# The last output rows in three column pieces: 256, then twice 128

## The chip, the core and the metric

The kernel runs on one core of a Trainium2 chip. A core has a matrix engine (PE, with the loading of its stationary operand shown apart as PEld), a vector engine (DVE), an activation engine (ACT), a general engine (POOL) and a queue engine for transfers (SP). PE writes its products into the banks of an accumulator memory (PSUM). ACT and DVE copy them from there into the core's working memory, which here is called evicting. Transfers between that memory and the chip's DRAM are issued from the queues of SP, ACT or POOL and carried out by 16 DMA engines that all queues share.

The metric is the device time of one execution in microseconds (us). The kernel before takes 514.16 us, the median of 3 runs (514.08 to 514.75).

## The reference

For 8 batches of 8 heads, 576 positions and 64 features the attention keeps only the scores that are within tau = 0.02 of a row's largest one. Its output, seen as 4608 rows of 512 features, goes through two dense layers:

```python
scores = scale * np.matmul(q, k.transpose(0, 1, 3, 2))
thresh = np.max(scores, axis=-1, keepdims=True) - tau
scores = np.where(scores >= thresh, scores, -1e9)
attn = np.exp(scores - np.max(scores, axis=-1, keepdims=True))
attn = attn / (np.sum(attn, axis=-1, keepdims=True) + 1e-09)
x = np.matmul(attn, v)                # then as 4608 rows of 512
h = x @ w_in                          # 512 -> 2048
g = np.maximum(0.01 * h, h)
out = g @ w_out                       # 2048 -> 512, float32
```

Inputs and outputs are float32. The kernel works with float16 operands in most matrix products.

## The kernel before

The attention runs over 16 steps of two head pairs (c), each of 9 tiles of queries (t). An order written out by hand, a list of letters for each tile, says in which sequence a tile's scores, its row maxima, its masking and the work of neighbouring steps are issued. The two dense layers are cut into small units that wait in a list called units. Letters of the order take units from the front of that list (the function work), so that PE has dense products to do while the vector engines treat the scores. What is left in the list after the last tile is issued by the last line of the kernel, work(len(units)).

A batch has 576 rows of output. 512 of them are treated per batch (push_main): 16 units of the first layer with 512 rows as moving columns, then 4 groups of second products. The 64 rows that remain, the tail, are treated for two batches together (push_tail): 2 x 64 = 128 rows. With i = 0, four units (h_unit) make the first product and its leaky ReLU, four groups of 128 columns each, and ACT writes them into gE, a tile of 16 blocks (j) of 128 x 128. With i = 1, four units (out_mm) make the second product: 16 matrix products, one per j, with gE's block j as the stationary operand and the 512 columns of w_out's block j as the moving one, all accumulated in one bank of PSUM. Batches 6 and 7 (b0 = B - 2) have the last tail, and its second product is the last thing that PE does.

Three sets of buffers matter. bank() gives one of two PSUM banks with the tag u, in turn. The attention's scores use two pairs of banks with the tag s. In working memory new_osb() gives one of two tiles for output (tag o), and the attention has two buffers with the tag far. A buffer is given again only after the last reader or writer of its former contents is done, and the needed waits are put in by the framework.

The last tail's eviction and its two stores stand on lines 392 to 397 and 435 to 438. ACT evicts columns 0 to 255, DVE columns 256 to 511 of the same bank. Both halves lie in one output tile, and then two stores are issued, one from SP for the 64 rows of batch 6 and one from ACT for the 64 rows of batch 7. A store of 64 rows moves 64 runs of 2 KB, 128 KB in all.

Of the kernel before, what the change touches and what calls it, by code (L numbers as in the profile page):

```python
# [9 lines left out]
FP32 = mybir.dt.float32  # L10
FP16 = mybir.dt.float16
OP = mybir.AluOpType
AF = mybir.ActivationFunctionType
# [3 lines left out]
def kernel(  # L17
# [10 lines left out]
    nc = tc.nc  # L28
    B, H, S, D = q.shape
# [6 lines left out]
    NJ = d_ff // 128  # L36
# [5 lines left out]
    sb = ctx.enter_context(tc.tile_pool(name="sb", bufs=1))  # L42
    ps = ctx.enter_context(tc.tile_pool(name="ps", bufs=1, space=bass.MemoryType.PSUM))
# [7 lines left out]
    w_out16 = sb.tile([128, NJ, d_model], FP16, name="wout16")  # L51
    gM = sb.tile([128, NJ, 512], FP16, name="gM")
    gEs = [sb.tile([128, NJ, 128], FP16, name=f"gE{i}") for i in range(2)]
# [15 lines left out]
    def bank():  # L69
        return ps.tile([128, 512], FP32, tag="u", bufs=2, name="u")  # L70
# [52 lines left out]
    def filler(n):  # L123
        if n > 0:
            t = bank()
            for _ in range(n):
                nc.tensor.matmul(out=t[:, :], lhsT=gM[:, 0, 0:128], rhs=gM[:, 0, :], start=True, stop=True,  # L127
                                 skip_group_check=True)
# [5 lines left out]
    def take(fs):  # L134
        r = list(fs)
        fs.clear()
        return r

    def run(fs):
        for f in fs:  # L140
            f()
# [221 lines left out]
    def h_unit(N, xs, g_out, j0, nj):  # L363

        assert all(("w", (j0 + nj - 1) // 4 * 4 + i) in was for i in range(4))
        t = bank()
        for j in range(nj):
            for gi in range(NG):
                nc.tensor.matmul(  # L369
                    out=t[:, ts(j, N)], lhsT=w_in16[:, gi, ts(j0 + j, 128)], rhs=xs[gi],  # L370
                    start=(gi == 0), stop=(gi == NG - 1), skip_group_check=True,
                )
        nc.scalar.activation(out=g_out, in_=t[:, 0:nj * N].rearrange("p (j n) -> p j n", j=nj),  # L373
                             func=AF.Prelu, bias=0.0, scale=1.0, alpha=0.01)
# [3 lines left out]
    def out_mm(key, g_in, part, osb, half, store):  # L378

        if part == 0:  # L380
            ot[key] = bank()
        t = ot[key]
        assert all(("w", 16 + j) in was for j in range(part * 4, part * 4 + 4))
        for j in range(part * 4, part * 4 + 4):
            nc.tensor.matmul(  # L385
                out=t[:, :], lhsT=g_in(j), rhs=w_out16[:, j, :],
                start=(j == 0), stop=(j == NJ - 1), skip_group_check=True,
            )
        if part == 3:
            del ot[key]  # L390
            o = osb()
            if key == (B - 2, "t"):
                nc.scalar.activation(out=o[:, half, 0:256], in_=t[:, 0:256], func=AF.Copy, bias=0.0, scale=1.0)  # L393
                nc.vector.tensor_copy(out=o[:, half, 256:512], in_=t[:, 256:512])  # L394
            else:
                nc.scalar.activation(out=o[:, half, :], in_=t[:, :], func=AF.Copy, bias=0.0, scale=1.0)  # L396
            store(o)

    units = []

    def new_osb():
        return sb.tile([128, 2, 512], FP32, tag="o", bufs=2, name="osb")
# [27 lines left out]
    def push_tail(b0, i):  # L430

        xs = [xE[g][:, b0:b0 + 2, :] for g in range(NG)]
        gE = gEs[b0 // 2 % 2]

        def store(o):
            for e in range(2):
                eng = nc.scalar if e == 1 and b0 == B - 2 else nc.sync
                eng.dma_start(out=out[ds((b0 + e) * S + 512, 64), :], in_=o[ds(e * 64, 64), 0, :])
        for j in range(0, NJ, 4):
            if i == 0:  # L440
                units.append((1, lambda j=j: h_unit(128, xs, gE[:, j:j + 4, :], j, 4)))
            else:
                units.append((0, lambda part=j // 4: out_mm(
                    (b0, "t"), lambda j: gE[:, j, :], part, new_osb, 0, store)))

    def work(n):
        for _ in range(min(n, len(units))):
            units.pop(0)[1]()

    with tc.manual_schedule():  # L450
        nc.scalar.preload_act_table_set("natural_log_exp_and_others")
        for i, tail in ((0, 0), (1, 0), (0, 1), (1, 1)):
# [6 lines left out]
            out=sel[:, :, :], in0=I32[:, 0:18].unsqueeze(2).to_broadcast([128, 18, 64]),  # L459
# [43 lines left out]
        for c in range(NC + 1):  # L503
            last = c == NC
            for t in range(NT):
                step = c * NT + t
                cl = c if c < 5 else 6 - c % 2
                ph = c % 2 * 9 + t

                def push():  # L510
                    if c % 4 == 2 and c > 2:
                        push_tail(c // 2 - 3, 1)
                    push_main(c // 2 - 1)
                    if c % 4 == 0:
                        push_tail(c // 2 - 2, 0)
                    if last:
                        push_tail(c // 2 - 2, 1)
                def target(x):
                    return x * NT + (6 if x == 2 else 6)
                nx = c // 2 * 2  # L520
                if step >= target(nx) or c < 2 and 0:
                    nx += 2
                def count():
                    global_ = sum(share[i % 18] for i in range(step, max(target(nx), step + 1)))
                    return (len(units) - credit) * share[ph] / global_
                n = None
                for o in orders[cl][t].split():
                    if o == "G":
                        if c > 1 and c % 2 == 0:
                            push()  # L530
                            nx = c // 2 * 2 + 2
                        continue
                    if n is None:
                        credit = min(credit, 1.0) + count()
                        n = min(int(credit + 0.01), len(units))
                        credit -= n
                        k1 = min(n, max(0, (n + up[cl][t]) // 2))
                        heads = [u[0] for u in units[:n]]
                    if o == "f":
                        filler([[1, 2, 3, 3, 3, 2, 2, 2, 2], [1, 3, 3, 2, 3, 3, 2, 3, 2], [1, 1, 4, 3, 2, 1, 0, 1, 0]][cl][t] if cl < 3 else 0)  # L540
                    elif o == "S" and not last:
                        s_mm(c, t)
                    elif o[0] == "V" and c > 0:
                        values(c - 1, int(o[1]))
                    elif o == "0" and not last:
                        s_max(c, t, 0, tau_f <= 8.0 and (t in d0[cl]))
                    elif o == "1" and not last:
                        direct = tau_f <= 8.0 and (t in d1[cl] or c > 2 and t not in d1n[cl] and not any(heads))
                        s_max(c, t, 1, direct)
                    elif o == "d" and c > 0:  # L550
                        sums_0(c - 1)
                    elif o == "r" and c > 0:
                        sums_1(c - 1)
                    elif o == "x" and c > 0:
                        sums_2(c - 1)
                    elif o == "T" and c > 0:
                        sums_3(c - 1)
                    elif o == "U":
                        work(k1)
                    elif o == "u":  # L560
                        work(n - k1 - (1 if "w" in orders[cl][t] and n > k1 else 0))
                    elif o == "w":
                        work(1 if n > k1 else 0)
                    elif o[0] == "P":
                        pi = {"a": (2 * c + 2, 0), "b": (2 * c + 2, 1), "c": (2 * c + 3, 0), "d": (2 * c + 1, 1), "e": (2 * c + 1, 0), "f": (2 * c + 3, 1)}[o[1]]
                        if pi[0] < NP:
                            prep(*pi)
                    elif o == "h":
                        run(take(due))
                    elif o[0] == "Q" and c > 0:  # L570
                        sums_4(c - 1, int(o[1]))
                    elif o == "M":
                        if prev is not None:
                            s_mask(*prev)
                            prev = None
                        if not last:
                            prev = (c, t)
                    elif o == "L":
                        run(take(soon))
                for f in plan.get(step, ()):  # L580
                    f()
# [36 lines left out]
```

## Time and profile before

| what | value |
|---|---|
| median of 3 runs | 514.16 us |
| time of the profiled execution | 513.46 us |
| its span, first to last instruction | 511.7 us |
| busy: PE, PEld | 501.1 us (98%), 272.1 us (53%) |
| busy: DVE, ACT, POOL | 412.8 us (81%), 427.8 us (84%), 205.1 us (40%) |
| granted PE clock | 0.999 |
| last tail, first products (L369, 64 of 128 columns) | from 500.11 us, 3.57 us |
| last tail, second products (L385, 16 of 512 columns) | from 503.68 us, 3.47 us |
| its evictions, ACT (L393) and DVE (L394) | 383 ns and 424 ns |
| its stores, from issue to landing | 2.3 us (SP), 2.6 us (ACT) |

Times are those of one profiled execution, counted from the start of its span. In the lines of the profile L385 is line 385 of the kernel, and out<-in names the tile that is written and the tiles that are read. SPq and ACTq are instructions that a queue works off, among them the issue of a transfer. A busy time of PE is modelled at its end, since its products are pipelined: the start times of a row of products, rather than the duration of one, tell its pace. The DMA share of a stretch is the mean busy share of the 16 DMA engines.

### The profile page before, as it was taken

The page shows a single profiled execution, that of the slowest core. Times are in us where ns is not written, and L with a number is a line of the kernel's source. Part 1 is how long each engine was busy: PE and PEld are TensorE (multiplying, and loading weights), DVE is VectorE, ACT ScalarE, POOL GpSimd, SP SyncE. Part 2 cuts the span into 40 slices and gives each one's busy share as a digit, 9 for nine tenths or more (in the row PEclk, how much of TensorE's full clock was granted, in tenths as well). Part 3 has the DMA queues.
Part 4 walks back from the last instruction along what each step waited for, and adds up shares of the span by engine and source line. Part 5 has one row for each costly group of instructions (what it writes and reads, how often), then busy time and mean ns, then how long its engine had stood idle before and what let it go on. Part 6 is the DMA issues. An engine that isn't in the chain of part 4 may idle for free.

```text
span 511.7 us, 13929 instructions
## 1 busy us (share of the span) xinstructions
PE 501.1 (98%) x5155; PEld 272.1 (53%) x5155; DVE 412.8 (81%) x1084; ACT 427.8 (84%) x775; POOL 205.1 (40%) x471
## 2 busy tenths in 40 slices
PE   8899999999999999999999999999999999999996
PEld 5455554555555475555555475555555575545444
DVE  5888898998899889998999889998999889981000
ACT  3898978988998988999898988999898988983712
POOL 5554567533642346323642346323642346320000
PEclk9999999999999999999999999999999999999999
DMA  8999999998999899979997899978997899764112
GB/s 183 176 214 199 209 200 185 177 176 146 193 182 151 139 183 181 189 139 156 173 194 135 159 183 191 160 141 153 166 201 138 158 193 146 105 94 88 41 42 61
DMA packets 260547, 80.60 MB, mean 158 GB/s; under 512 B 248704, under 2 KB 257920, under 8 KB 260480
## 3 DMA queue, kind: packets, MB, share of 16 engines
q1 hardware_dynamic: 234032, 70.68, 78.5%
q0 software_dynamic: 26368, 8.92, 16.7%
q8 instruction: 40, 0.66, 0.6%
q14 instruction: 27, 0.22, 0.1%
q10 hardware_dynamic: 80, 0.13, 0.1%
HBM read 36.70 MB, written 9.44 MB: 90 GB/s over the span
## 4 chain that ended last, share of the span: by engine, by line
PE 90%; DVE 3%; ACT 3%; issue 2%; DMA 1%; POOL 1%; DVEq 0%; ACTq 0%; POOLq 0%
PE u L385 25%; PE u L369 25%; PE s L210 23%; PE A L343 8%; PE A L160 3%; PE u L127 2%; PE A L327 2%; PE A L152 2%; DVE sn L235 1%; DVE W L268 1%; DMA V<-in_v_dram 1%; ACT e L245 1%; ACT far L251 1%; ACT W L255 1%; POOL nth L240 0%
## 5 line engine op out<-in xcount | busy, mean ns | idle before, releaser
L235 DVE TENSOR_SCALAR_CACHE_REDUCE sn<-s 128x576 f32<-128x576 f32 x288 | 208.0, 754 | 42.2 <-PE s L210 40.2
L240 POOL TENSOR_SCALAR nth<-nmx 128x1 f32<-128x1 f32 x288 | 114.4, 397 | 215.8 <-DVE sn L235 200.2
L245 ACT ACTIVATE e<-sn,nmx 128x576 f16<-128x576 f32 x191 | 143.9, 770 | 22.8 <-DVE sn L235 22.0
L268 DVE SCALAR_TENSOR_TENSOR W<-sn,nth,e 128x576 f16<-128x576 f32 x191 | 151.8, 814 | 1.8 <-ACT e L245 1.1
L210 PE MATMUL s<-x,x 64*128 64x288 f16 (+1 forms) x1440 | 130.6, 304 | 1.5 <-DVE sn L235 1.4
L369 PE MATMUL u<-xT,win 128*128 128x512 f16 x512 | 123.4, 380 | 0.0
L385 PE MATMUL u<-wout,gM 128*128 128x512 f16 x512 | 121.7, 380 | 0.0
L210 PEld LDWEIGHTS <-x 64*128 64x128 f16 (+1 forms) x1560 | 60.4, 96 | 55.4 <-issue 43.3
L369 PEld LDWEIGHTS <-win 128*128 128x128 f16 x768 | 58.6, 98 | 55.5 <-issue 10.5
L251 ACT ACTIVATE far<-sn,nth 128x576 f32<-128x576 f32 x97 | 75.1, 774 | 14.6 <-POOL nth L240 12.8
L373 ACT ACTIVATE gM<-u 128x512 f16<-128x512 f32 x128 | 72.3, 590 | 6.4 <-PE u L369 6.3
L385 PEld LDWEIGHTS <-gM 128*128 128x128 f16 x512 | 45.0, 98 | 53.1 <-issue 6.5
L255 ACT ACTIVATE W<-far 128x576 f16<-128x576 f32 x97 | 66.3, 683 | 3.1
L107 POOL DMA_DIRECT2D V<-in_v_dram x80 | 50.3, 635 | 2.7 <-DVE sn L235 1.0
L343 PE MATMUL A<-wT,V 128*64 128x288 f16 x640 | 45.4, 288 | 0.0
L188 DVE SCALAR_TENSOR_TENSOR x<-A,x 128x512 f16<-128x512 f32 (+1 forms) x52 | 39.2, 755 | 3.9 <-ACT x L185 3.4
L343 PEld LDWEIGHTS <-V 128*64 128x64 f16 x640 | 33.6, 109 | 11.0 <-issue 7.8
L396 ACT ACTIVATE osb<-u 128x512 f32<-128x512 f32 x35 | 20.5, 587 | 17.3 <-PE u L385 16.7
L185 ACT ACTIVATE x<-A 128x512 f16<-128x512 f32 (+1 forms) x52 | 33.0, 635 | 0.3
L356 DVE TENSOR_TENSOR xT<-A,rc 128x576 f16<-128x576 f32 x32 | 24.2, 756 | 8.2 <-PE A L343 8.1
L394 DVE COPY osb<-u 128x256 f32<-128x256 f32 x1 | 0.4, 424 | 35.3 <-ACT osb L393 35.3
L210 PEld LDWEIGHTS s<-x,x 64*128 64x128 f32 x192 | 20.6, 185 | 12.2 <-DVE sn L235 6.3
(48 smaller groups left out, 330.5 us busy)
## 6 DMA issues: line engine op xcount, KB each, us to landing
nat<-in_q_dram SPq DMA_DIRECT2D x32, 256.0 KB, 4.0
nat<-in_k_dram SPq DMA_DIRECT2D x32, 256.0 KB, 4.2
out_dram<-osb SPq DMA_DIRECT2D x32, 256.0 KB, 3.6
V<-in_v_dram POOLq DMA_DIRECT2D x64, 64.0 KB, 4.3
wT<-W SPq DMA_TRANSPOSE x144, 4.3
win<-in_moe_w_in_dram POOLq DMA_DIRECT2D x16, 128.0 KB, 4.4
wout<-in_moe_w_out_dram POOLq DMA_DIRECT2D x16, 128.0 KB, 4.2
nat<-in_q_dram SPq DMA_DIRECT2D x32, 32.0 KB, 3.7
```

Of the source, the lines that this page charges most:

```text
L107: nc.gpsimd.dma_start(out=Vs[b % 2][r0:r0 + 64, :, e, c0:c0 + n, :].rearrange("p g c d -> p g (c d)"), in_=rows_.rearrange("g (p c) d -> p ...
L210: nc.tensor.matmul(out=out[h][po, half, 0:288], lhsT=qk[p][i][a][r, cols], rhs=qk[p][1][b][r, ds(half * 288, 288)], start=(ti == 0), stop= ...
L235: nc.vector.tensor_scalar(out=sn[:, h, :].rearrange("p (a b) -> p a b", a=2), in0=s_[:, :, 0:288], scalar1=-BS, scalar2=None, op0=OP.mult, ...
L240: nc.gpsimd.tensor_scalar(out=nth[:, h:h + 1], in0=nmx[:, h:h + 1], scalar1=1.0, scalar2=tau_f, op0=OP.mult, op1=OP.add,)
L245: nc.scalar.activation(out=e[:, h, :], in_=sn[:, h, :], func=AF.Exp, bias=nmx[:, h:h + 1], scale=-1.0,)
L251: nc.scalar.activation(out=far[:, :], in_=sn[:, h, :], func=AF.Prelu, bias=nth[:, h:h + 1], scale=-1.0, alpha=BIG,)
L255: nc.scalar.activation(out=w[:, ds(h * 576, 576)], in_=far[:, :], func=AF.Exp, bias=0.0, scale=1.0, accum_out=dens[c][:, 2 * t + h:2 * t + ...
L268: nc.vector.scalar_tensor_tensor(out=w[:, ds(h * 576, 576)], in0=sn[:, h, :], scalar=nth[:, h:h + 1], in1=e[:, h, :], op0=OP.is_le, op1=OP ...
L343: nc.tensor.matmul(out=t[ds(h * 64, 64), half, 0:288], lhsT=vb[:, g, h, kb, :], rhs=wT[:, 4 * h + kb, ds(e * 576 + half * 288, 288)], star ...
L369: nc.tensor.matmul(out=t[:, ts(j, N)], lhsT=w_in16[:, gi, ts(j0 + j, 128)], rhs=xs[gi], start=(gi == 0), stop=(gi == NG - 1), skip_group_c ...
L373: nc.scalar.activation(out=g_out, in_=t[:, 0:nj * N].rearrange("p (j n) -> p j n", j=nj), func=AF.Prelu, bias=0.0, scale=1.0, alpha=0.01)
L385: nc.tensor.matmul(out=t[:, :], lhsT=g_in(j), rhs=w_out16[:, j, :], start=(j == 0), stop=(j == NJ - 1), skip_group_check=True,)
```

## The change

The second product of the last tail becomes a function of its own, last_tail, which stands in the list of units as one entry. It works by columns in two rounds. The first round makes columns 0 to 255 for all 16 blocks j in a bank of tag u. ACT evicts them into a tile of tag o, and SP issues their store. The second round makes columns 256 to 383 and 384 to 511 in turns, block by block, in two banks of tag s, one in each pair. ACT evicts the first of them and DVE the second, each into a buffer of tag far. ACT issues the store of its own piece and SP that of DVE's piece. Every store covers the 128 rows of both batches: on the DRAM side it is a pattern of 2 batches x 64 rows x 256 or 128 columns, in working memory 128 partitions x 256 or 128 columns.

The branch for the last tail in out_mm and the choice of ACT's queue in push_tail go away, and all other tails and main rows keep their code.

```diff
         if part == 3:
             del ot[key]
             o = osb()
-            if key == (B - 2, "t"):
-                nc.scalar.activation(out=o[:, half, 0:256], in_=t[:, 0:256], func=AF.Copy, bias=0.0, scale=1.0)
-                nc.vector.tensor_copy(out=o[:, half, 256:512], in_=t[:, 256:512])
-            else:
-                nc.scalar.activation(out=o[:, half, :], in_=t[:, :], func=AF.Copy, bias=0.0, scale=1.0)
+            nc.scalar.activation(out=o[:, half, :], in_=t[:, :], func=AF.Copy, bias=0.0, scale=1.0)
             store(o)
...
         def store(o):
             for e in range(2):
-                eng = nc.scalar if e == 1 and b0 == B - 2 else nc.sync
-                eng.dma_start(out=out[ds((b0 + e) * S + 512, 64), :], in_=o[ds(e * 64, 64), 0, :])
+                nc.sync.dma_start(out=out[ds((b0 + e) * S + 512, 64), :], in_=o[ds(e * 64, 64), 0, :])
...
+    def last_tail():
+
+        b0 = B - 2
+        gE = gEs[b0 // 2 % 2]
+        rows_ = out.rearrange("(b r) n -> b r n", b=B)[b0:b0 + 2, 512:576, :]
+        for pieces in (((0, 256),), ((256, 128), (384, 128))):
+            if len(pieces) == 1:
+                ts_ = [bank()[:, 0:256]]
+            else:
+                ts_ = [ps.tile([128, 2, 512], FP32, tag="s", bufs=2, name="s")[:, 0, 0:n] for _, n in pieces]
+            for j in range(NJ):
+                for t, (c0, n) in zip(ts_, pieces):
+                    nc.tensor.matmul(
+                        out=t, lhsT=gE[:, j, :], rhs=w_out16[:, j, ds(c0, n)],
+                        start=(j == 0), stop=(j == NJ - 1), skip_group_check=True,
+                    )
+            for m, (t, (c0, n)) in enumerate(zip(ts_, pieces)):
+                o = sb.tile([128, 576], FP32, tag="far", bufs=2, name="far")[:, 0:n] if n == 128 else new_osb()[:, 0, 0:n]
+                if m == 0:
+                    nc.scalar.activation(out=o, in_=t, func=AF.Copy, bias=0.0, scale=1.0)
+                else:
+                    nc.vector.tensor_copy(out=o, in_=t)
+                (nc.scalar if n == 128 and m == 0 else nc.sync).dma_start(out=rows_[:, :, ds(c0, n)], in_=o)
...
                     if last:
-                        push_tail(c // 2 - 2, 1)
+                        units.append((0, last_tail))
```

## The prediction

> **What bounds the kernel now.** I read the page first, then the chain of waits in order of time, then the groups of the last stage, and last the DMA view of the final stores. The page says that TensorE (PE) is busy for 98% of the span. The chain of the last 22 us shows what the edit can touch:
>
> ```profile
> 489.96 10.14 PE u L385 x47
> 500.11 3.57 PE u L369 x64
> 503.68 3.47 PE u L385 x16
> 507.15 0.03 ACTq L393
> 507.17 0.04 issue
> 507.22 0.39 ACT osb L393
> 507.61 0.02 issue
> 507.63 0.42 DVE osb L394
> ```
>
> The columns are start, duration and work. PE ends at 507.15 us. After it the two half evictions run one behind the other and end at 508.05, although they are on different engines. The timeline then has only the two stores, and the waits of SP's queue show what the program's end waits for:
>
> ```profile
> 508.09 0.47 SPq L438 DMA_DIRECT2D out_dram<-osb  x1
> 508.09 0.56 ACTq L438 DMA_DIRECT2D out_dram<-osb  x1
> ...
> SPq L613 <- DMA out_dram<-osb: 1.7, 1, 1.7
> ```
>
> So the end is PE's end, the evictions, the data of the last store, and a fixed rest. The DMA view from 508.0 to 510.8 (40 slices of 0.07 us) gives the data its place:
>
> ```profile
> DMA  0000000000000000085997944959999630000000
> ...
> DMA packets 160, 0.26 MB, mean 94 GB/s; under 512 B 32, under 2 KB 32, under 8 KB 160
> ...
> q1 hardware_dynamic: 80, 0.13, 22.7%
> q10 hardware_dynamic: 80, 0.13, 12.3%
> ```
>
> The first busy slice is the 18th and the last the 33rd: data moves from 509.19 to 510.31 us, 1.10 us after the issue and for 1.12 us. From 510.31 to the span's end at 511.70 there are 1.39 us in which nothing moves. Each queue (q1 is SP's, q10 ACT's) shows 80 packets for 64 rows of 2 KB: 64 of data and 16 tiny ones, one completion for each of the 16 DMA engines. The shares give what a 2 KB packet takes on its engine: 0.227 x 16 x 2.8 us / 64 = 159 ns on SP's queue, 0.123 x 16 x 2.8 / 64 = 86 ns on ACT's.
>
> For shorter packets there is the stretch from 200 to 240 us, nearly all 256-byte packets:
>
> ```profile
> DMA packets 22801, 6.42 MB, mean 161 GB/s; under 512 B 22542, under 2 KB 22542, under 8 KB 22795
> ...
> q1 hardware_dynamic: 21798, 6.13, 88.1%
> ```
>
> 0.881 x 16 x 40 us / 21798 = 26 ns each. The groups by shape give the evictions and the small matmuls:
>
> ```profile
> L369 PE MATMUL u<-xE,win 128*128 128x128 f16 x64 | 3.7, 219 | 0.0
> ...
> L312 ACT ACTIVATE row<-A 128x128 f16<-128x128 f32 x16 | 4.4, 277 | 0.3 <-PE A L309 0.3
> ...
> L393 ACT ACTIVATE osb<-u 128x256 f32<-128x256 f32 x1 | 0.4, 383 | 2.9 <-PE u L385 2.9
> ...
> L394 DVE COPY osb<-u 128x256 f32<-128x256 f32 x1 | 0.4, 424 | 35.3 <-ACT osb L393 35.3
> ```
>
> **The change part by part.** Before the last 16 products nothing moves on any engine: putting one entry into the list in place of four only changes how the tail of an otherwise finished list is handed out.
>
> *PE.* Sixteen products of 512 columns (3.47 us, 217 ns each) become sixteen of 256 and thirty-two of 128. The first take half, 108 ns, 1.74 us in all; the weight load of 98 ns still fits beneath one. The thirty-two go by the chain's 64 products of 128 columns, each with a load of its own, in 3.57 us: 56 ns each, 1.79 us. PE ends its first part at 505.42 and its second at 507.20: 0.05 us lost. The last quarter of gE is now read at 503.68 + 12 x 0.108 = 504.98 and written at 503.71 + 0.60 = 504.31; of that cover 0.67 us is left, and lateness beyond it would add one for one. The banks with tag s and the buffers with tag far were last used in the attention stage (far by 461.4 us), so nothing waits for them.
>
> *Evictions.* The first piece costs ACT 0.38 us from 505.49 to 505.87, under PE's second part. ACT's next instruction waits for PE at 507.2, so nothing queues behind it. The last two pieces run side by side from about 507.21 (ACT) and 507.27 (DVE): as the program is built, DVE's copy waits for PE alone, where before it waited for ACT too. ACT takes 0.28 by the 128x128 row. For DVE no PSUM copy of 128 columns exists: the bounds are 0.23 (its 128x128 cast in SBUF, 226 ns) and the 0.42 of 256 columns; 256 to 512 columns costs it 424 to 687 ns in the nearest rows, so 0.29. ACT's store goes out at 507.53, SP's at 507.60 in place of 508.09: 0.49 us gained up to the issue.
>
> *The first store.* SP issues it at 505.91. SP has nothing else, having issued its last main store by 501.9, and is free by 506.5 (issues take 0.47 to 0.67 us), well before its second store. The one instruction queued behind the wait for ACT is that store. Its data starts 1.10 us later, at 507.01.
>
> *The data.* This decides. The stores of before are lists of 64 rows, outermost on both sides. The new ones are built as 2 x 64 x 256 and 2 x 64 x 128 on the DRAM side: outermost are the two batches, and between their rows lies a jump, so they can't be one list. No plain copy in this trace has so small an outermost count; all have 64 or 128, and spread evenly over 16 engines. What 2 does is bounded by the rows on one side (16 engines) and by one engine per outermost slice on the other (2 engines). I take 2: each engine gets equal shares of the outermost dimension in all that the trace shows, and 2 has only two shares to give. Then the first store is 64 packets of 1 KB on either engine, and each final store 64 packets of 512 bytes on either, with both final stores on the same pair, behind the first.
>
> Price of a packet: in proportion to the 86 ns of 2 KB, 1 KB takes 43 ns and 512 bytes 21; by a line through 26 ns at 256 bytes and 86 at 2 KB, 52 and 35. I take the middle, 47 and 28, since the trace has packets at both paces. One engine then works 64 x 47 ns = 3.0 us plus 128 x 28 ns = 3.6 us, 6.6 us from 507.01: data ends at 513.6 against 510.31. That is +3.3 us. The 0.49 won at the issue is gone with it: the final stores find the pair still busy with the first until 510.0. Ends: at 43 and 21 ns 5.4 us of data, +2.1; at half and a quarter of the 159 ns (79 and 40) 10.2 us, +6.9.
>
> The Trainium skill, page "DMA: Bandwidth & Descriptors", section "Why a DMA increments its semaphore by 16 and not by 1", says that the descriptor generator takes the slowest dimension that isn't 1 on each side and uses the largest number of engines up to 16 that divides both; by it this sum is the one with two engines, and by the spread of this trace's rows it would be the one of the first rival. The 16 completions for 64 rows agree with it, but no run so far has a smaller count.
>
> *Sum.* The profiled execution took 513.46 us (span 511.70, 1.76 around it), 0.70 below the median of 514.16. Span +3.3 gives 515.0, execution 516.8, and on the median 517.5 us, 0.6% slower.
>
> **The rivals.**
>
> *All sixteen engines share each store.* For it speaks that every transfer of this trace does. Then each engine has 16 final packets, 16 x 28 ns = 0.45 us, against 1.12 before; the first store is over by about 507.5. Data ends near 509.2 to 509.3 (half of 1.12 gives 0.56): 1.05 us gained, 513.1 us; with the data no shorter only 0.5 is gained, 513.7. It decides by the number of engines: the whole work is 13.2 us of engine time from 507.01, so four engines would end at 510.3, just as before; above four it gains, below it loses. Against it: the shape of the stores.
>
> *Two engines for each store, but another pair for ACT's queue.* Then SP's pair has 64 x 47 + 64 x 28 ns = 4.8 us, ending at 511.8: +1.5, 515.7 us. The two stores of before shared all 16 engines, which says nothing on pairs. The same page, in the same section, puts such a transfer on the lowest-numbered engines, which is against this rival; no run here shows it.
>
> *Small products bound by the weight load.* At 98 ns each the thirty-two take 3.1 us in place of 1.8. With 16 engines the gain of 1.05 turns into +0.3, 514.5 us. Against it stand the 64 like products at 56 ns. With two engines it is hidden: the pair is busy with the first store.
>
> **How the numbers follow.** 0.2% (1.03 us) is about what a measurement of this kernel can tell from no change. Chances: one shared pair 0.77, two pairs 0.06, sixteen engines 0.14, loads as the bound 0.03. The time is that of the first, 517.5. The range goes from just under the two-pair case, 515.4, to the upper packet price, 514.16 + 6.9 = 521.1, and leaves out the last two cases. The sixteen-engine case lies across the bound of 0.2%, so it is split. Faster 0.08, same 0.09, slower 0.83.
>
> **What would show it.** ACT's queue: 130 packets (128 and 2 completions) if two engines carry it, 144 if sixteen do. In the slices after 507.0 the DMA share would stay near 2/16, tenths of 1, for some 6 us, where before it reached 9. PE's last product should end at 507.2, the final evictions should overlap, the issues should stand near 507.5 and 507.6. The prediction is wrong if the DMA share after 508.6 rises above half, or if a pair of engines moves short packets much faster or slower than 28 ns.

## The result and the profile after

The changed kernel takes 517.17 us (median of 4 runs, 517.05 to 517.95) against 514.12 (513.82 to 514.75): 3.05 us more, a ratio of 1.0056 with a 95% interval of 1.0042 to 1.0071. The profiled execution took 517.24 us, its span is 515.5.

The chain of waits of the changed kernel (start, duration, work) and the timeline behind it:

```profile
500.53 3.57 PE u L369 x64
504.11 1.75 PE u L453 x16
505.86 1.80 PE s L453 x32
507.65 0.02 issue
507.68 0.29 DVE far L462
```

```profile
506.35 0.62 SPq L463 DMA_DIRECT2D out_dram<-osb  x1
507.62 0.28 ACT L460 ACTIVATE far<-s 128x128 f32<-128x128 f32 x1 [1.30 <-PE s L453]
507.68 0.29 DVE L462 COPY far<-s 128x128 f32<-128x128 f32 x1 [34.87 <-PE s L453]
507.93 1.44 ACTq L463 DMA_DIRECT2D out_dram<-far  x1
508.00 0.53 SPq L463 DMA_DIRECT2D out_dram<-far  x1
```

The compute side did what the change says. The two small pieces cost PE 1.75 + 1.80 us against 3.47, and the last two evictions overlap. SP's last store is issued 0.34 us after PE's last product (507.66), where before 0.94 us lay between. The loss comes after that. The DMA view of the changed kernel from 505 to 515 us, in 40 slices of 0.25 us:

```profile
DMA  0000000000011111011111111111111111111000
GB/s 0 0 0 0 0 0 0 0 0 0 25 33 45 29 33 33 16 16 29 41 49 49 45 49 45 45 43 43 43 45 43 43 43 43 43 45 33 0 0 0
DMA packets 390, 0.26 MB, mean 26 GB/s; under 512 B 6, under 2 KB 390, under 8 KB 390
...
q1 hardware_dynamic: 260, 0.20, 6.9%
q10 hardware_dynamic: 130, 0.07, 2.2%
```

While data moves, for about 6.7 us (507.6 to 514.2), the digit is 1 at most: the share stays below 2 tenths. Of the 390 packets only 6 are completions: two for each of three stores. ACT's queue has 130, 128 of data and 2 completions, where the store of before had 64 and 16. A row of the table of stages (length, then the engines' busy times, granted clock, DMA share, GB/s) shows a pair of engines at work, 2/16 being 0.125. The share may lie somewhat above that where packets of one engine overlap in time, as with the 0.14 of most stages after 511:

```profile
510.50:511.00 0.50, 0.00 (x0) 0.00 (x0) 0.00 (x0) 0.00 (x0) 0.00 (x0) 1.00 0.13 47
```

All of the 3.8 us by which the two spans differ can be placed. PE begins the last tail's first products 0.42 us later, which no part of the change touches (this point moved between 500.1 and 503.0 from run to run below). PE's second products take 0.08 us more. From PE's last product to the end of the span it is 7.84 us in place of 4.55, 3.29 more. That last figure, here called the **ending**, is the clean measure of what follows, since the part of the kernel before the last tail is nearly the same in all runs, yet varies in length by more than the effects sought. It is read from the one profiled execution of each run, and spans are given to 0.1 us.

### The profile page after: what moved, and what is told of

Same layout as the page of the kernel before. It is cut to its first block, busy times and chain, and to the rows that moved or that the text cites. A ratio compares the mean times of both kernels' runs of the same rounds, so it can differ in the third digit from the quotient of the medians.

```text
span 515.5 us, 13993 instructions
## 1 busy us (share of the span) xinstructions
PE 501.5 (97%) x5187; PEld 274.0 (53%) x5187; DVE 412.6 (80%) x1084; ACT 428.1 (83%) x776; POOL 205.3 (40%) x471
## 4 chain that ended last, share of the span: by engine, by line
PE 89%; DVE 3%; ACT 3%; issue 2%; POOL 1%; DMA 1%; DVEq 0%; ACTq 0%; POOLq 0%
PE u L369 25%; PE u L385 25%; PE s L210 23%; PE A L343 8%; PE A L160 3%; PE u L127 2%; PE A L327 2%; PE A L152 2%; DVE sn L235 1%; DVE W L268 1%; DMA V<-in_v_dram 1%; ACT e L245 1%; ACT far L251 1%; ACT W L255 1%; POOL nth L240 0%
```

## The experiments

The theory is the prediction's: the outermost dimension of a store decides how many DMA engines carry it. The rivals are that short packets or more stores are the cost, that the jump between the two batches is, or that PE's small products are.

**Each store cut by batch.** Six stores with 64 rows outermost, the packets unchanged:

```diff
-                (nc.scalar if n == 128 and m == 0 else nc.sync).dma_start(out=rows_[:, :, ds(c0, n)], in_=o)
+                for e in range(2):
+                    (nc.scalar if n == 128 and m == 0 else nc.sync).dma_start(out=rows_[e, :, ds(c0, n)], in_=o[ds(64 * e, 64), :])
```

> Each of the three stores is cut in two, one for each batch: six stores of 64 rows, with 64 outermost on both sides and packets of the same 1 KB and 512 bytes. Theory (the outermost count of 2 confines a store to two DMA engines): all 16 engines work, the last store is issued near 508.1 us and its data ends near 509.5 where before it ended at 510.3, so 0.6 to 1.0 us less than before. Rival (short packets or more stores are the cost): stays 2 to 4 us above before.

Measured: 513.98 us, ratio to before 0.9991 (0.9975 to 1.0007). The ending is 4.24 us (PE's last product at 507.66, span 511.9). The 3.3 us are gone with the same short packets, so those are not the cause, nor is the number of stores, which doubled. The DMA view from 506 to 512 us (slices of 0.15 us) has digits up to 9, and ACT's queue has 160 packets: 128 of data and 16 completions for each of two stores.

```profile
DMA  0000000001591058300006361536200000000000
...
q10 hardware_dynamic: 160, 0.07, 4.5%
```

The gain over before, 0.31 us by the ending and none that can be told by the time, is half of the least that was expected. The data ends near 510.3, not 509.5. A likely reason, which no run tested alone, is that the timeline has two issues in a row on either queue:

```profile
507.94 1.45 ACTq L464 DMA_DIRECT2D out_dram<-far  x2
508.00 1.10 SPq L464 DMA_DIRECT2D out_dram<-far  x2
```

**One store of two batches in the kernel before.** Nothing of the columns, only the shape of the final store:

```diff
         def store(o):
+            if b0 == B - 2:
+                rows_ = out.rearrange("(b r) n -> b r n", b=B)[b0:b0 + 2, 512:576, :]
+                nc.sync.dma_start(out=rows_, in_=o[:, 0, :])
+                return
```

> The kernel before, with its evictions one behind the other; only its two final stores of 64 x 512 become one store of 2 x 64 x 512 from SP. Theory: 64 packets of 2 KB on either of two engines, 64 x 84 ns = 5.4 us of data in place of 1.1, so 4.0 to 4.5 us above before. Rival (the columns with their short packets make the loss): within 0.5 us of before.

Measured: 519.45 us, ratio 1.0103 (1.0074 to 1.0131), which is 5.3 us more (the medians differ by 4.8), and an ending of 9.82 us, 5.27 above before. The shape alone makes a loss, and a larger one than the changed kernel's. Its DMA view from 508 to 518 us (slices of 0.25 us):

```profile
DMA  0000000012020200201101111111111110000000
...
DMA packets 130, 0.26 MB, mean 26 GB/s; under 512 B 2, under 2 KB 2, under 8 KB 130
...
q1 hardware_dynamic: 130, 0.26, 8.2%
```

130 packets again: 128 and 2 completions. The price was a fifth above the forecast: 0.082 x 16 x 10 us / 128 is 102 ns per packet, not 84. In the first 2.5 us there are slices in which the pair does next to nothing; from 513.25 us on the same view has 49 to 57 GB/s, and 49 GB/s over two engines is one packet of 2 KB every 84 ns. The forecast was thus the pace of the steady part, and the slow start is what it left out.

**Four and eight engines.** The kernel before with its two stores. POOL lays the 64 rows of each batch in another order, so that the DRAM side is U x 64/U x 512; U is 4 or 8:

```diff
+    xL = [sb.tile([128, 2, 4, 16], FP16, name=f"xL{g}") for g in range(NG)]
...
+                nc.gpsimd.tensor_copy(out=xL[g][:, b - (B - 2), :, :], in_=last_rows.rearrange("p (v u) -> p u v", u=4))
...
+                    rows_ = rows_.rearrange("(v u) n -> u v n", u=4)
```

> The kernel before with its two stores of 64 rows, whose rows POOL has put in another order, so that the DRAM side of each is 4 x 16 x 512. Theory (the engines of a store are counted by its outermost dimension): four engines, 32 packets of 84 ns each, 2.7 us of data where before it was 1.1: 1.4 to 1.8 us above before, and 68 packets on ACT's queue in place of 80. Rival (only two or sixteen engines are possible, or only the jump between batches matters): 4 us above or the same.

> As the run with 4 x 16 x 512, with 8 x 8 x 512. Theory: eight engines, 16 packets of 84 ns each, 1.35 us of data: 0.1 to 0.5 us above before, 72 packets on ACT's queue. Rival as there.

Measured: U = 4 takes 517.86 us, ratio 1.0053 (1.0036 to 1.0069), ending 7.82 us; U = 8 515.87, 1.0023 (1.0005 to 1.0041), ending 5.61. ACT's queue has 68 and 72 packets: four and eight completions. The page's list of queues for U = 8 (U = 4 follows below):

```profile
q10 hardware_dynamic: 72, 0.13, 0.1%
```

The count of engines thus follows the outermost dimension, with no jump between batches inside a store, and that rival falls. The sizes were missed: 3.27 and 1.06 us above before by the ending, where 1.4 to 1.8 and 0.1 to 0.5 were expected. The DMA views tell the larger part of why. For U = 4, from 510 to 518 us:

```profile
q1 hardware_dynamic: 68, 0.13, 7.8%
q10 hardware_dynamic: 68, 0.13, 4.2%
```

0.078 x 16 x 8 us / 64 = 156 ns for a packet of SP's store, which comes first, and 84 ns for one of ACT's. The expectation had priced both at 84, though the kernel before had shown 159 and 86. With 156 and 84 the engine time is 16 x 156 + 16 x 84 ns = 3.8 us in place of 2.7. The data ran for 4.4 us (512.2 to 516.6); the other 0.6 us are gaps, whose cause is open.

**The first store alone cut by batch,** in the changed kernel:

```diff
+                if n == 128:
+                    (nc.scalar if m == 0 else nc.sync).dma_start(out=rows_[:, :, ds(c0, n)], in_=o)
+                else:
+                    for e in range(2):
+                        nc.sync.dma_start(out=rows_[e, :, ds(c0, n)], in_=o[ds(64 * e, 64), :])
```

> The changed kernel, but its first store alone is cut in two by batch, so that it uses 16 engines; the two final stores keep their 2 x 64 x 128. Theory (all stores share one pair, the first ahead of the last two): the pair begins the final stores near 509.1 and needs 128 x 27 ns = 3.5 us, so data ends 1.6 us earlier than in the changed kernel: 1.3 to 1.8 us above before. Rival (each queue has a pair of its own, or the final stores alone set the end): the pairs would need 64 x 27 ns = 1.7 us, so 0.4 us below to 0.2 above before; or no gain against the changed kernel, 3 us above before.

Measured: 517.27 us, 2.6 us above before, ratio 1.0051 (1.0031 to 1.0072), which by itself can't be told from the changed kernel's and misses the 1.3 to 1.8 us that were expected. Its seven times spread over 3.3 us, so the trace has to decide. The ending is 6.44 us (PE's last product 507.76, span 514.2): 1.40 below the changed kernel's and 1.89 above before, just outside the expected range. The last data moves at 512.6, 4.8 us after PE's last product, where in the changed kernel it is 6.5 (514.2). So the first store did hold up the last two, and queues with a pair each (an ending near or below that of before) are excluded. The DMA view from 506 to 513 us (slices of 0.175 us) has both parts side by side:

```profile
DMA  0000000005811840000111111111111111111000
GB/s 0 0 0 0 0 0 0 0 0 152 193 30 47 205 117 6 0 0 0 29 41 47 41 47 41 32 41 47 29 41 44 44 41 47 41 41 47 9 0 0
```

The first store reaches a share of 8 tenths and is over before 509. In the last two stores together the digit stays at 1, at 41 to 47 GB/s in most slices, for 3.3 us, although they come from two queues: they share one pair. The changed kernel's own trace says the same. From 512.65 to 513.15 us both queues move short packets, from 513.5 to 514 only ACT's does:

```profile
q10 hardware_dynamic: 22, 0.01, 7.4%
q1 hardware_dynamic: 21, 0.01, 7.1%
```

```profile
q10 hardware_dynamic: 43, 0.02, 14.5%
```

That is 43 packets in half a microsecond for two queues as for one.

**Columns with the stores of before.** Pieces and evictions of the changed kernel into one tile, then the two stores of 64 x 512:

```diff
+        whole = new_osb()
...
-                o = sb.tile([128, 576], FP32, tag="far", bufs=2, name="far")[:, 0:n] if n == 128 else new_osb()[:, 0, 0:n]
+                o = whole[:, 0, ds(c0, n)]
...
+        for e in range(2):
+            (nc.scalar if e else nc.sync).dma_start(out=rows_[e], in_=whole[ds(64 * e, 64), 0, :])
```

> Columns and evictions as in the changed kernel, all three pieces into one output tile, then the two stores of 64 x 512 of before, once both last evictions are done. Theory: the issue moves from 508.1 to 507.6 relative to the same end of PE's first products, and 0.3 to 0.6 us are gained against before; nothing of the loss stays. Rival (the small products or the two banks cost more than the trace of the changed kernel says): no gain, 0 to 1 us above before.

Measured: 514.72 us, ratio 0.9996 (0.9982 to 1.0011), no difference that can be told. The ending is 4.09 us (PE's last product 509.91, span 514.0), 0.46 below before, just what the side by side evictions should bring. The pieces lie in one output tile as before, and ACT (from 509.88) and DVE (from 509.99) still evict at the same time. So it was not the shared output tile that kept the two evictions of before apart; what is no longer shared is the bank, which no run tested by itself.

**The rows in turns of the batches.** One store over both batches may use all engines if its outermost dimension is the 64 rows. PE reads the tail's columns in that order:

```diff
+        if b0 == B - 2:
+            xs = [x.rearrange("p b s -> p s b") for x in xs]
...
-        rows_ = out.rearrange("(b r) n -> b r n", b=B)[b0:b0 + 2, 512:576, :]
+        rows_ = out.rearrange("(b r) n -> b r n", b=B)[b0:b0 + 2, 512:576, :].rearrange("b s n -> s b n")
```

> The tail's 128 rows are taken in another order, row by row with the two batches in turns, so that the DRAM side of each store is 64 x 2 x columns; still three stores with the same packets and the same jump between batches. Theory: 64 outermost gives 16 engines, ACT's queue shows 144 packets in place of 130, and the time is 0.7 to 1.2 us below before. Rival (the jump between the batches or the single store over both is slow): 2 to 4 us above before, as in the changed kernel.

Measured: 517.78 us, ratio 1.0053 (1.0036 to 1.007): a loss of the size that the rival foretold, but in another place. The ending is 3.62 us, the shortest of all (3.66 and 3.67 follow below), and ACT's queue has 144 packets. The chain shows where the time went:

```profile
500.79 7.85 PE u L369 x64
508.63 1.75 PE u L455 x16
510.38 1.80 PE s L455 x32
```

The 64 first products take 7.85 us in place of 3.57: their moving columns alternate between the two batches and lie 64 elements apart. To take that away, POOL now writes the order when it collects the rows, which it does anyway (454 ns for a copy in either order):

```diff
+    xL = [sb.tile([128, 64, 2], FP16, name=f"xL{g}") for g in range(NG)]
...
+            last_rows = x[:, 0:64] if e else x[:, 512:576]
+            if b < B - 2:
+                nc.gpsimd.tensor_copy(out=xE[g][:, b, :], in_=last_rows)
+            else:
+                nc.gpsimd.tensor_copy(out=xL[g][:, :, b - (B - 2)], in_=last_rows)
...
+        if b0 == B - 2:
+            xs = [x[:, :, :] for x in xL]
```

> The rows of the last tail again in turns of the two batches, so that each store is 64 x 2 x columns, but now POOL writes them in that order when it collects them, and PE reads 128 columns side by side. Theory (the shape of the moving operand, not the store, made the row order of the run before slow): the 64 first products take 3.6 us again, not 7.9; from PE's last product to the end of the span 3.6 us, against 4.55 before and 7.85 in the changed kernel; the time 0.7 to 1.2 us below before. Rival (the row order costs elsewhere, or POOL's copies do): at or above before.

Measured: 513.47 us, ratio 0.9977 (0.9964 to 0.9989); a second comparison on another chip gave 513.37 us and 0.9981 (0.9969 to 0.9993).

> Columns, with the rows in turns of the batches by POOL, on the same chip as the run beside it. Theory: 3.67 us from PE's last product to the end, 0.7 to 1.2 us below before. Rival: the first comparison was chance, and the time lies within 0.3 us of before.

The ending is 3.67 us in the first run and 3.66 in the second. The chain and the DMA view from 506 to 511 us (slices of 0.125 us) of the first:

```profile
500.11 3.57 PE u L374 x64
503.69 1.75 PE u L460 x16
505.43 1.80 PE s L460 x32
```

```profile
DMA  0000000002997000000000396960000000000000
GB/s 0 0 0 0 0 0 0 0 0 106 328 344 254 17 0 0 0 0 0 0 0 0 94 291 185 279 189 12 0 0 0 0 0 0 0 0 0 0 0 0
```

Both the first store and the last two reach the digit 9 (90% or more) and are over in 0.5 to 0.75 us. The jump between the batches and the single store over both are still there, and the loss is not: the outermost count is what made it. This version is faster than the kernel before, by 0.9 us by the ending, and by 1.2 and 1.0 us by the ratios of the two comparisons (their medians differ by 1.23 and 0.71).

**Rows in turns without the columns.** The kernel before with its evictions one behind the other, and a store of 64 x 2 x 256 for each half:

```diff
+            if b0 == B - 2:
+                rows_ = out.rearrange("(b r) n -> b r n", b=B)[b0:b0 + 2, 512:576, :].rearrange("b s n -> s b n")
+                for m in range(2):
+                    (nc.scalar if m else nc.sync).dma_start(out=rows_[:, :, ds(256 * m, 256)], in_=o[:, 0, ds(256 * m, 256)])
+                return
```

> The kernel before with its 16 products of 512 columns and its two evictions one behind the other; the last tail's rows lie in turns of the two batches, as POOL writes them, and each evicted half of 256 columns gets a store of its own, 64 x 2 x 256, from SP after ACT's half and from ACT's queue after DVE's. Theory (the stores set the end, and the last eviction alone delays them): the last store is issued 0.94 us after PE's last product and has 8 packets of 1 KB on each of 16 engines, 0.4 us, so 3.8 us from PE's last product to the end of the span, against 4.55 before and 3.67 with columns and turns; 0.5 to 0.9 us below before. Rival (the gain of columns with turns comes from PE's columns and the parallel evictions): 4.4 us or more, within 0.2 us of before.

Measured: 514.57 us, ratio 0.9999 (0.9984 to 1.0013). The ending is 4.07 us (509.93 to 514.0), between the theory's 3.8 and the rival's 4.4, so neither was right: stores in turns bring 0.48 us without the columns, just short of the 0.5 expected, and the columns another 0.40 on top. Neither half alone can be told from before by its time; together they can.

## Why the prediction was right, point by point

- *PE:* 0.05 us lost was forecast, 0.08 were measured. The 32 small products ran at 56 ns each (1.80 us), not at the 98 ns of a weight load.
- *Evictions and issue:* ACT 0.28 and DVE 0.29 us, as priced, and in parallel. The final issues came 0.60 us earlier after PE's last product on SP (0.34 for 0.94), where the forecast had 0.54.
- *Two engines:* this step decided, and it held. Two completions per store in the changed kernel; 2, 4, 8 and 16 when the outermost count is 2, 4, 8 and 64. The Trainium skill's rule, page "DMA: Bandwidth & Descriptors", section "Why a DMA increments its semaphore by 16 and not by 1", agrees in every one of these runs.
- *One pair for both queues:* held as well. The run with the first store cut shows both final stores inside a share of 2/16.
- *Price of a packet:* right as an average, and partly by luck. 512 bytes were forecast at 28 ns; 0.022 x 16 x 10 us / 128 is 27.5 on ACT's queue. For the first store's 1 KB packets 47 ns were forecast. What is left on SP's queue after its 128 short packets at 27.5 is 0.069 x 16 x 10 - 3.5 = 7.5 us, 59 ns each, so the forecast was a fifth too low. Against that, packets of one engine overlap: the pair shows 7.3 us of work each in 6.7 us. The time itself splits otherwise: the first store moved for about 3.5 us (507.6 to 511.1), where 3.0 were forecast, and the last two for 3.1 us (511.1 to 514.2), where 3.6 were. The GB/s row above shows why. From 510 us on the pair moves 49 GB/s of 1 KB packets, one every 42 ns on either engine, and later 43 GB/s of 512-byte packets, one every 24 ns; that is near the cheap end of the forecast (43 and 21), and at this pace all the data would have taken some 5.7 us. Before 509.75 it moves 16 to 45 GB/s. This slow start is in no term of the forecast and makes up the other 1 us.
- *Sum:* +3.3 us was forecast; the endings differ by 3.29, the medians by 3.05. The mechanism (two engines, one pair for both queues, the first store ahead of the last two) is what the runs show. That the size came out so exactly is luck: the middle between two prices, taken because the trace has packets at both paces, made up for a slow start that no term had. With the cheap end alone the forecast would have been +2.1.

The break-even of four engines that the first rival named was not tried for this kernel. The runs with U = 4 and U = 8 only suggest that it lies higher: there eight engines still lose 1.06 us against sixteen, with the first store's packets, of 2 KB there, at the slow pace.

## What to carry to other kernels

Before a store is merged over a short outer dimension, look which dimension is outermost on its DRAM side: with 2 outermost only 2 of 16 DMA engines worked here, and 256 KB that took 1.1 us took 6.7. The completions in the packet count of a queue tell the number of engines at a glance (80 for 64 rows on 16 engines, 130 for 128 rows on 2). Put a count outermost that all 16 engines can share (64 did it here; 16 itself and loads were not tried), and if rows have to be laid in another order for that, let an engine with spare time write the order rather than have PE read across it.

## What the runs showed that was not expected

- PE's 64 products of 128 moving columns took 7.85 us, 123 ns each, when neighbouring columns lay 64 elements (128 bytes) apart, and 3.57 us, 56 ns each, when they lay side by side. In the kernel before they lie side by side too: the 64 columns of batch 7 follow those of batch 6 in the tile xE. The Trainium skill, page "SBUF — State Buffer", section "Door 1: The DMA port swizzle (why `[64,N]` ≈ `[32,N]`)", says that consecutive accesses to the same 16-byte line run at the full rate and that each access that crosses to a new line pays a penalty; the two figures agree with that, and no run here varied the distance to test the 16 bytes.
- A packet of 2 KB took 138 to 160 ns for the first of two stores and 84 to 86 for the second, on 16, 8 and 4 engines; on two engines, with one store, 102 on average and 84 in the steady part. Stores on few engines started slowly: gaps and low rates for about 2.2 us in the changed kernel, 2.5 us in the run with one store and 1.6 us with U = 4. The last two stores of the run with the first store cut did not: they reach 41 GB/s in their second slice. What holds the first packets up was not settled: in the runs with the rows in turns by POOL the first store, 1 KB packets from all 128 partitions, reaches the digit 9 within two slices of 0.125 us.
- ACT's queue needed 1.23 to 1.51 us to issue a store when it used 2, 4 or 8 engines and 0.56 to 0.73 us with 16, while SP's issue of a like store beside it took 0.47 to 0.71. In the changed kernel and with U = 4 it did not set the end: ACT's first packet moved 2.6 and 2.0 us after its issue was over, while SP's packets were still moving. With U = 8 only 0.7 us lay between, so there a part of the loss may come from the late issue. The cause of the long issue is open.
